# Attention and a convolved feed-forward layer on one core: early steps of three engines put in another order

## The chip, the cores and the metric

The kernel runs on one core of a Trainium2 chip. A core has a matrix engine (TensorE, PE in the profile; its weight loads are shown apart as PEld), three engines for work by element (VectorE = DVE, ScalarE = ACT, GpSimd = POOL) and a sequencer that issues most transfers (SyncE = SP). Each engine takes its instructions in one order and stops at an instruction whose inputs are not there. The metric is the device time of one execution in microseconds (us); the kernel before takes 469.8 us, the median of 469.11, 469.8 and 470.95.

## The reference

Attention in chunks of 64 rows for 8 batches, 8 heads, 576 rows and 64 columns a head, then a feed-forward layer with a convolution of three taps along the sequence and a sigmoid gate:

```python
scores = scale * np.matmul(q_c, k_c.transpose(0, 1, 2, 4, 3))     # chunks of 64 rows
scores = scores - np.max(scores, axis=-1, keepdims=True)
attn = np.exp(scores)
attn = attn / (np.sum(attn, axis=-1, keepdims=True) + 1e-09)
x = np.matmul(attn, v_c)            # heads side by side: 8 x 576 x 512
...
h = np.maximum(x @ w_in, 0.0)       # 512 -> 1024
conv_out[t] = sum of conv_w[k] * h[t - 1 + k] for k in 0, 1, 2
gate = 1.0 / (1.0 + np.exp(-conv_out))
return h * gate @ w_out             # 1024 -> 512
```

The weights come as 64-bit numbers; all results are 32-bit.

## The kernel before

**Attention by tiles.** The 4608 rows are 36 tiles of 128 (t0 to t35). For each of the early ones the loads bring q and k (`load_rows`, L129 and L136) and v (L186). TensorE transposes q and k into PSUM (`t_pe`, L198 and L203, two halves), a copy brings them to SBUF (`t_copy`: L77 on ScalarE, L79 on VectorE), TensorE forms the scores (L250) in a pair of PSUM banks called sx. VectorE takes the maximum and subtracts it (`s_max` L260, `s_sub` L264), ScalarE does the exponential (`s_exp` L269), VectorE the sum (`s_sum` L273), an addition of 1e-9 (`s_eps`, L277 on ScalarE or L279 on VectorE) and the reciprocal (`s_rec` L282); `s_norm` (L322) multiplies, on VectorE or GpSimd. TensorE transposes the result (`p_pe` L329), a copy follows (`p_copy`), and `attn_v` (L342) writes the attention output into the sx pair. It is split into a high and a low part for the next product: `x_hi` (L397, ScalarE) and `x_lo` (L401, VectorE).

**The feed-forward layer by units.** 384 rows make a unit. For each of eight blocks of 128 columns of w_in, `mm1` (L411) makes 12 matmuls (high by high, low by high, high by low) into one of six PSUM banks b0 to b5. `h_relu` (L419) makes the ReLU there, `c_mid` (L449, ScalarE) and `c_left`, `c_right` (L454, VectorE) add the three taps, `c_sig` (L465, ScalarE) is the gate and `c_mul` (L484, VectorE) multiplies; only then is the bank free for another block or a transpose. In the names here c_mul[0,2] is unit 0, block 2. The last product, by w_out, is done with seven products of sums of quarters (`product` L515), whose right sides `f_hi`, `f_lo` (L502) and `f_sum` (L505) prepare.

**The weights.** Six loads for w_in (wi0a to wi3) and four for w_out (wo0 to wo3) go through two slots of SBUF, w0 and w1 (L547). Three steps turn a 64-bit number into a 32-bit one: `w_scale` (L561, ScalarE), `w_shift` (L565, VectorE) and `w_words` (L570, VectorE), and after the last the slot is free for the next load. `w_hi` (L77 or L79) and `w_left` (L574) split the result into its two parts; for w_out there are also `w_diff` (L592 to L594), `w_lo_q` (L587) and, for the sums of quarters, `w_lo_d` (L600).

**What sets the order.** Each of these is a step with an engine, a cost, a list of the steps that it follows, and sometimes other engines that can do it. Two tables of numbers decide. `moved_` (L968) holds 4 x step + n: that step goes to its n-th other engine. `order_` (L997) is a list of all steps; a planner goes through it, gives out the buffers and banks in that order and works out when each step begins on its engine. The steps are then written out in the order of these begins, and each engine's instructions are tied to that order. Where the plan sees TensorE idle before 110 us, it puts filler matmuls on an identity (L1161). A step of GpSimd that uses the SBUF port it shares with VectorE is made to wait for the step of VectorE that `order_` names ahead of it, if the plan has the two at one time.

## Time and profile before

| | before |
|---|---|
| median of 3 runs | 469.8 us |
| profiled execution | 470.28 us, span 468.5 us |
| busy: PE, DVE, ACT, POOL | 456.2, 409.6, 263.7, 283.5 us |
| granted clock of PE | 1.00 in all slices |
| DMA | 64.32 MB, 137 GB/s over the span |

The span is the time from the first to the last instruction that the profiler shows; the profiled execution's own time is 1.8 us longer. In the page, a row of a timeline is a start, a length, an engine and a line, what is written and read, how many instructions; in brackets the idle time of the engine just before, and whose end ended it as far as the profile can tell.

### The profile page before, as it was taken

The page shows a single profiled execution, that of the slowest core. Times are in us where ns is not written, and L with a number is a line of the kernel's source. Part 1 is how long each engine was busy: PE and PEld are TensorE (multiplying, and loading weights), DVE is VectorE, ACT ScalarE, POOL GpSimd, SP SyncE. Part 2 cuts the span into 40 slices and gives each one's busy share as a digit, 9 for nine tenths or more (in the row PEclk, how much of TensorE's full clock was granted, in tenths as well). Part 3 has the DMA queues.
Part 4 walks back from the last instruction along what each step waited for, and adds up shares of the span by engine and source line. Part 5 has one row for each costly group of instructions (what it writes and reads, how often), then busy time and mean ns, then how long its engine had stood idle before and what let it go on. Part 6 is the DMA issues. An engine that isn't in the chain of part 4 may idle for free.

```text
span 468.5 us, 13076 instructions
## 1 busy us (share of the span) xinstructions
PE 456.2 (97%) x5287; PEld 444.3 (95%) x5287; DVE 409.6 (87%) x771; ACT 263.7 (56%) x544; POOL 283.5 (61%) x256
## 2 busy tenths in 40 slices
PE   7899899999999999999999999999999999999996
PEld 7779798999999999999999999999999999999996
DVE  2899999999999899989788889998989987977784
ACT  3589988756646555564444564455556453542641
POOL 0344768847686654979678967755856643448221
PEclk9999999999999999999999999999999999999999
DMA  7999999999896839687987495741215101100012
GB/s 223 248 305 306 246 149 218 158 177 209 147 158 175 191 95 178 126 158 180 181 182 182 109 172 111 169 128 33 58 35 157 25 24 29 40 17 31 22 46 91
DMA packets 184320, 64.32 MB, mean 137 GB/s; under 512 B 155564, under 2 KB 175044, under 8 KB 184260
## 3 DMA queue, kind: packets, MB, share of 16 engines
q1 hardware_dynamic: 184260, 63.48, 62.7%
q8 instruction: 42, 0.69, 0.6%
q14 instruction: 18, 0.15, 0.1%
HBM read 50.88 MB, written 23.59 MB: 159 GB/s over the span
## 4 chain that ended last, share of the span: by engine, by line
PE 80%; DVE 9%; DMA 5%; ACT 2%; issue 1%; SPq 1%; POOL 1%; DVEq 0%; ACTq 0%; POOLq 0%
PE b_ps L411 36%; PE b_ps L515 36%; DVE gt L454 2%; PE sx_ps L250 2%; PE sx_ps L342 2%; PE z_ps L342 2%; DMA v<-in_v 1%; DMA w<-in_moe_w_out 1%; DVE f L502 1%; DMA qk<-in_k 1%; DMA w<-in_moe_conv_w 1%; DVE wt L570 1%; PE z_ps L250 1%; PE b_ps L329 1%; SPq L129 1%
## 5 line engine op out<-in xcount | busy, mean ns | idle before, releaser
L515 PE MATMUL b_ps<-wo_h,f 128*128 128x256 f32 x1008 | 190.9, 282 | 0.4 <-DVE wt L533 0.3
L515 PEld LDWEIGHTS b_ps<-wo_h,f 128*128 128x128 f32 x1008 | 158.8, 188 | 2.0 <-issue 0.5
L515 PE MATMUL b_ps<-wo_l,f 128*128 128x256 f32 x504 | 141.2, 280 | 0.0
L454 DVE SCALAR_TENSOR_TENSOR gt<-b_ps,cw,gt 128x384 f32<-128x384 f32 (+3 forms) x208 | 116.4, 576 | 11.2 <-ACT gt L449 9.1
L502 POOL TENSOR_TENSOR f<-gt,f 128x512 fp32r<-128x512 f32 x67 | 86.4, 1294 | 45.5 <-ACT f L77 16.3
L515 PEld LDWEIGHTS b_ps<-wo_l,f 128*128 128x128 f32 x504 | 94.9, 188 | 0.0
L411 PE MATMUL b_ps<-x_h,wi_h 128*128 128x386 f32 (+2 forms) x384 | 84.6, 342 | 0.0
L411 PE MATMUL b_ps<-x_l,wi_h 128*128 128x386 f32 (+2 forms) x384 | 83.3, 339 | 0.0
L411 PE MATMUL b_ps<-x_h,wi_l 128*128 128x386 f32 (+2 forms) x384 | 83.1, 338 | 0.0
L465 ACT ACTIVATE gt<-gt 128x384 f32<-128x384 f32 (+2 forms) x96 | 49.9, 524 | 54.5 <-DVE gt L454 54.2
L411 PEld LDWEIGHTS b_ps<-x_l,wi_h 128*128 128x128 f32 x384 | 68.8, 188 | 0.0
L411 PEld LDWEIGHTS b_ps<-x_h,wi_l 128*128 128x128 f32 x384 | 68.6, 188 | 0.0
L449 ACT ACTIVATE gt<-b_ps,cw 128x384 f32<-128x384 f32 (+2 forms) x104 | 56.5, 556 | 20.6 <-DVE b_ps L421 18.5
L411 PEld LDWEIGHTS b_ps<-x_h,wi_h 128*128 128x128 f32 x384 | 65.5, 188 | 1.0 <-ACT gt L449 0.2
L505 POOL TENSOR_TENSOR gt<-gt 128x512 f32<-128x512 f32 x41 | 52.8, 1295 | 15.3 <-DVE gb L505 6.0
L484 DVE SCALAR_TENSOR_TENSOR gt<-gt,b_ps 128x192 f32<-128x192 f32 (+2 forms) x120 | 47.2, 410 | 8.8 <-ACT gt L465 8.5
L419 ACT ACTIVATE b_ps<-b_ps 128x386 f32<-128x386 f32 (+2 forms) x79 | 37.6, 479 | 28.2 <-PE b_ps L411 27.0
L79 POOL CAST f<-gt 128x512 fp32r<-128x512 f32 x43 | 26.9, 625 | 21.2 <-PE b_ps L515 18.0
L527 ACT ACTIVATE wt<-b_ps 128x256 f32<-128x256 f32 x54 | 20.6, 381 | 29.8 <-PE b_ps L515 29.7
L77 ACT CAST f<-gt 128x512 fp32r<-128x512 f32 x44 | 26.9, 617 | 14.8 <-PE b_ps L515 8.5
L502 POOL TENSOR_TENSOR f<-gb,f 128x512 fp32r<-128x512 f32 x18 | 23.2, 1294 | 17.9 <-DVE f L502 9.9
L220 DVE STREAM_TRANSPOSE qkT<-qk 128x1024 f32<-128x1024 f32 (+1 forms) x30 | 33.4, 1121 | 0.0
(99 smaller groups left out, 585.6 us busy)
## 6 DMA issues: line engine op xcount, KB each, us to landing
out<-wt SPq DMA_DIRECT2D x36, 256.0 KB, 2.7
qk<-rows SPq DMA_DIRECT2D x24, 320.0 KB, 5.8
rows<-in_q SPq DMA_DIRECT2D x12, 576.0 KB, 8.1
rows<-in_k SPq DMA_DIRECT2D x12, 576.0 KB, 7.8
qk<-rows SPq DMA_DIRECT2D x24, 256.0 KB, 4.6
v<-in_v SPq DMA_DIRECT2D x21, 256.0 KB, 5.0
w<-in_moe_w_out SPq DMA_DIRECT2D x4, 1024.0 KB, 6.5
wt<-wt SPq DMA_DIRECT2D x48, 64.0 KB, 2.0
```

Of the source, the lines that this page charges most:

```text
L77: nc.scalar.copy(out=out, in_=in_)
L79: ENG[eng].tensor_copy(out=out, in_=in_)
L220: nc.vector.transpose(out=to[:, :, i:i + n], in_=of[:, :, o:o + n])
L411: nc.tensor.matmul(h_ps[:, 0:w], lhsT=wt[:, f // 2, kt, P * (f % 2):P * (f % 2) + P], rhs=xt[:, u % NX, kt, 0:w], start=n == 0, stop=n == ...
L419: nc.scalar.activation(out=h, in_=h, func=AF.Relu)
L449: nc.scalar.mul(out=g, in_=h, mul=cw[:, FT + f:FT + f + 1])
L454: nc.vector.scalar_tensor_tensor(out=g, in0=h, scalar=w, in1=g, op0=ALU.mult, op1=ALU.add)
L465: nc.scalar.activation(out=g, in_=g, func=AF.Tanh, scale=0.5)
L484: nc.vector.scalar_tensor_tensor(out=o, in0=g, scalar=1.0, in1=hv, op0=ALU.add, op1=ALU.mult)
L502: ENG[eng].tensor_tensor(out=part(st, 1), in0=quarter(*src), in1=part(st, 0).bitcast(F32), op=ALU.subtract)
L505: ENG[eng].tensor_tensor(out=quarter(*out_), in0=quarter(*a), in1=quarter(*b), op=op)
L515: nc.tensor.matmul(o, lhsT=part(ft, a)[:, j, :], rhs=w[:, i, j, :], start=first and n == 0, stop=n == 3 * FT // 2 - 1, skip_group_check=True)
```

## The change

Only the two tables change, 18 lines of `moved_` and 43 of `order_`; the diff begins

```diff
     moved_ = [
-        89, 113, 141, 165, 186, 225, 353, 505, 793, 801, 817, 969, 977, 1045, 1121, 1129, 1197, 1205, 1465,
...
+        65, 89, 93, 165, 186, 225, 353, 457, 465, 793, 801, 817, 933, 969, 1009, 1045, 1093, 1121, 1129, 1197,
...
     order_ = [
-        84, 85, 103, 87, 88, 0, 104, 18, 1, 86, 2, 105, 3, 90, 4, 5, 89, 91, 6, 122, 92, 19, 20, 7, 106, 107, 8,
...
+        84, 85, 87, 86, 103, 104, 18, 0, 1, 88, 105, 2, 4, 3, 90, 91, 19, 106, 107, 5, 6, 92, 109, 89, 93, 122,
```

The steps of TensorE and the loads keep their order. Other engines take: on VectorE instead of ScalarE one half of t_copy of t3, t4 and t5, and on ScalarE instead of VectorE one of t2 and s_eps of t1; s_norm of t1 goes from GpSimd to VectorE and that of t3 the other way; the first w_left (wi0b) goes from GpSimd to VectorE and that of wi1b the other way; w_hi of wi0a and wi1a change between ScalarE and GpSimd. Some steps of tiles 9 and 10 and of the groups of f near them (s_eps, s_norm, f_lo, f_hi, p_copy, one h_relu) change engines too. The 30 filler matmuls stay 30: three of them go from in front of attn_v of t2 to an earlier place, and three of 512 columns from in front of unit 1's first mm1 to in front of attn_v of t4. VectorE's two lists have the same work behind them at unit 1's c_mul of block 0, but for one s_sum (t8, now later) and the steps that changed engines; behind it the orders differ in short stretches, the last of them near tile 11. Three places follow.

**ScalarE, tiles 2 and 3.** Before; `qkT_266` is tile 3's q and k, of which the two rows are the two halves of t_copy; L561 on `w1_103` is w_scale of wi0a, on `w0_102` that of the load behind it, wi1a; L269 is s_exp of t0 and t1, and p_all is p_copy of t0:

```order
L269 ACTIVATE wt_202<-wt_202 128x512
L269 ACTIVATE wt_246<-wt_246 128x512
L77 COPY qkT_233<-b4_ps_111 128x2x2x2x64
L561 ACTIVATE wt_284<-w1_103 128x512
L77 COPY qkT_266<-b0_ps_107 128x2x2x2x64
L561 ACTIVATE wt_320<-w0_102 128x512
L77 COPY p_all_95<-b1_ps_108 128x512
L77 COPY qkT_266<-b2_ps_109 128x2x2x2x64
```

and now:

```order
L77 COPY qkT_232<-b4_ps_111 128x2x2x2x64
L77 COPY qkT_232<-b5_ps_112 128x2x2x2x64
L269 ACTIVATE wt_263<-wt_263 128x512
L561 ACTIVATE wt_298<-w1_103 128x512
L277 ACTIVATE z_300<-z_300 128x8
L77 COPY p_all_95<-b1_ps_108 128x512
L77 COPY qkT_266<-b2_ps_109 128x2x2x2x64
L561 ACTIVATE wt_330<-w0_102 128x512
```

Before, the second L561 (wi1a) stood ahead of p_copy of t0 and of the second half of tile 3's t_copy; now it stands behind both. The first half of that t_copy is gone from the list, since VectorE has it, and a second row of t2's t_copy (`b5_ps`) and s_eps of t1 (L277) have come.

**ScalarE, tiles 3 to 6.** Before; `w1_103` is the slot of the load wi2, `p_all<-b4_ps` is p_copy of t3, the two qkT rows are tile 6's t_copy, and L277 is s_eps of t4:

```order
L77 COPY p_all_95<-b5_ps_112 128x512
L77 COPY p_all_95<-b4_ps_111 128x512
L397 CAST x_h_90<-sx_ps_75 128x4x128
L397 CAST x_h_90<-sx_ps_75 128x4x2
L269 ACTIVATE wt_493<-wt_493 128x512
L77 COPY qkT_545<-b0_ps_107 128x2x2x2x64
L77 COPY qkT_545<-b1_ps_108 128x2x2x2x64
L561 ACTIVATE wt_591<-w1_103 128x1024
L277 ACTIVATE z_589<-z_589 128x8
L269 ACTIVATE wt_593<-wt_593 128x512
```

and now, with the first h_relu (L419) as the last row:

```order
L77 COPY p_all_95<-b5_ps_112 128x512
L269 ACTIVATE wt_508<-wt_508 128x512
L397 CAST x_h_90<-sx_ps_75 128x4x128
L397 CAST x_h_90<-sx_ps_75 128x4x2
L561 ACTIVATE wt_588<-w1_103 128x1024
L77 COPY p_all_95<-b4_ps_111 128x512
L77 COPY qkT_546<-b2_ps_109 128x2x2x2x64
L277 ACTIVATE z_586<-z_586 128x8
L77 COPY qkT_546<-b1_ps_108 128x2x2x2x64
L269 ACTIVATE wt_590<-wt_590 128x512
L419 ACTIVATE b3_ps_110<-b3_ps_110 128x384
```

L561, w_scale of wi2, came behind p_copy of t3 and both halves of tile 6's t_copy; it now stands ahead of the three, behind x_hi of t2 (L397).

**VectorE, the last weights.** Before, L600 is w_lo_d of wo0, and `wt_968` is the weight tile of wo1 (L565 w_shift, L570 w_words), with s_max and s_sub of t7 (L260, L264) and a c_mul (L484) between:

```order
L454 SCALAR_TENSOR_TENSOR gt_92<-b2_ps_109,cw_94,gt_92 128x383
L600 TENSOR_TENSOR wo_l_89<-wt_833,wo_h_88 128x4x256
L565 TENSOR_SCALAR wt_968<-wt_968 128x1024
L260 TENSOR_REDUCE m_988<-sx_ps_75 128x2x4
L484 SCALAR_TENSOR_TENSOR gt_92<-gt_92,b3_ps_110 128x256
L484 SCALAR_TENSOR_TENSOR gb_93<-gt_92,b3_ps_110 128x127
L264 TENSOR_TENSOR wt_1006<-sx_ps_75,m_988 128x2x4x64
L570 SCALAR_TENSOR_TENSOR wt_968<-w1_103,wt_968 128x1024
```

and now, first around w_words of wo1 (`wt_896`):

```order
L454 SCALAR_TENSOR_TENSOR gt_92<-b1_ps_108,cw_94,gt_92 128x383
L454 SCALAR_TENSOR_TENSOR gt_92<-b0_ps_107,cw_94,gt_92 128x383
L454 SCALAR_TENSOR_TENSOR gt_92<-b3_ps_110,cw_94,gt_92 128x382
L570 SCALAR_TENSOR_TENSOR wt_896<-w1_103,wt_896 128x1024
L454 SCALAR_TENSOR_TENSOR gt_92<-b3_ps_110,cw_94,gt_92 128x383
L484 SCALAR_TENSOR_TENSOR gt_92<-gt_92,b1_ps_108 128x256
L484 SCALAR_TENSOR_TENSOR gb_93<-gt_92,b1_ps_108 128x127
L260 TENSOR_REDUCE m_994<-sx_ps_75 128x2x4
```

and further on, around w_lo_d of wo0; L273 is s_sum of t7, L260 s_max of t8, L282 s_rec of t7, the L484 rows are c_mul of unit 1's blocks 4 and 2, and L502 is the first f_lo:

```order
L273 TENSOR_REDUCE z_1096<-wt_1059 128x8
L600 TENSOR_TENSOR wo_l_89<-wt_822,wo_h_88 128x4x256
L454 SCALAR_TENSOR_TENSOR gt_92<-b2_ps_109,cw_94,gt_92 128x193
L454 SCALAR_TENSOR_TENSOR gt_92<-b2_ps_109,cw_94,gt_92 128x192
L260 TENSOR_REDUCE m_1136<-sx_ps_75 128x2x4
L282 RECIPROCAL z_1096<-z_1096 128x8
L484 SCALAR_TENSOR_TENSOR gb_93<-gt_92,b2_ps_109 128x1
L484 SCALAR_TENSOR_TENSOR gt_92<-gt_92,b2_ps_109 128x192 x2
L484 SCALAR_TENSOR_TENSOR gb_93<-gt_92,b5_ps_112 128x1
L484 SCALAR_TENSOR_TENSOR gt_92<-gt_92,b5_ps_112 128x192 x2
L502 TENSOR_TENSOR f0_1066<-gt_92,f0_1066 128x512
```

w_words of wo1 has moved ahead of s_max and s_sub of t7, and w_lo_d of wo0 from two rows in front of w_shift of wo1 to behind s_sum of t7. The first f_lo, which stood ahead of c_mul of blocks 4 and 2, now follows them.

## Rows read from the trace of the kernel before

**Rows 1.** Page: busy time by engine; chain that ended last, by engine

```profile
PE 456.2 (97%) x5287; PEld 444.3 (95%) x5287; DVE 409.6 (87%) x771; ACT 263.7 (56%) x544; POOL 283.5 (61%) x256
...
PE 80%; DVE 9%; DMA 5%; ACT 2%; issue 1%; SPq 1%; POOL 1%; DVEq 0%; ACTq 0%; POOLq 0%
```

**Rows 2.** Windows: us, busy time by engine (instructions), granted clock, DMA share, GB/s

```profile
12.00:36.00 24.00, 21.24 (x452) 18.14 (x452) 21.45 (x44) 16.74 (x31) 10.47 (x11) 1.00 0.96 278
36.00:48.00 12.00, 12.00 (x132) 11.62 (x131) 11.73 (x21) 11.23 (x24) 5.72 (x7) 1.00 1.03 307
48.00:60.00 12.00, 10.50 (x176) 9.14 (x175) 12.00 (x24) 11.29 (x25) 7.43 (x7) 1.00 0.98 218
60.00:84.00 24.00, 23.01 (x194) 21.83 (x193) 24.00 (x62) 20.80 (x46) 18.39 (x16) 1.00 1.10 194
84.00:468.00 384.00, 379.79 (x4228) 374.73 (x4226) 337.45 (x618) 198.95 (x416) 240.65 (x211) 1.00 0.56 115
```

**Rows 3.** Timeline of PE, 14 to 35 us: start, length, tile, idle before

```profile
21.32 0.46 PE L250 MATMUL sx_ps<-qkT 64*64 64x64 f32 x16 [1.21 <-ACT qkT L77]
...
26.44 1.13 PE L198 MATMUL b_ps<-ident,qk 128*64 128x128 f32 x16 [0.59 <-DMA qk<-in_k]
...
30.99 0.74 PE L1161 MATMUL b_ps<-ident_r 128*128 128x256 f32 x3
```

**Rows 4.** Timeline of ACT, 14 to 37 us

```profile
19.60 0.67 ACT L561 ACTIVATE wt<-w 128x512 f32<-128x512 f32 x1 [2.33 <-DMA w<-in_moe_w_in]
...
20.64 0.63 ACT L77 COPY qkT<-b_ps 128x512 f32<-128x512 f32 x1
...
32.42 0.66 ACT L397 CAST x_h<-sx_ps 128x512 fp32r<-128x512 f32 x2 [0.42 <-PE sx_ps L342]
...
34.89 1.14 ACT L561 ACTIVATE wt<-w 128x1024 f32<-128x1024 f32 x1
...
36.85 0.47 ACT L419 ACTIVATE b_ps<-b_ps 128x384 f32<-128x384 f32 x1
```

**Rows 5.** DMA issues of wi3 (21.6 us) and wi2 (27.4 us): KB, us to landing

```profile
w<-in_moe_w_in SPq DMA_DIRECT2D x1, 1024.0 KB, 8.0
...
w<-in_moe_w_in SPq DMA_DIRECT2D x1, 1024.0 KB, 6.9
```

**Rows 6.** Timeline of PE, 51 to 62 us

```profile
58.65 0.69 PE L342 MATMUL sx_ps<-p_all,v 64*64 64x64 f32 x32 [1.04 <-ACT gt L465]
...
60.15 0.95 PE L1161 MATMUL b_ps<-ident_r 128*128 128x512 f32 x3
```

**Rows 7.** Timeline of DVE, 44 to 80 us

```profile
48.90 1.23 DVE L570 SCALAR_TENSOR_TENSOR wt<-w,wt 128x1024 uint32<-128x1024 uint32 x1
...
63.23 1.21 DVE L600 TENSOR_TENSOR wo_l<-wt,wo_h 128x1024 fp32r<-128x1024 f32 x1
...
66.69 1.51 DVE L570 SCALAR_TENSOR_TENSOR wt<-w,wt 128x1024 uint32<-128x1024 uint32 x1
...
77.06 0.60 DVE L484 SCALAR_TENSOR_TENSOR gt<-gt,b_ps 128x192 f32<-128x192 f32 x2
```

**Rows 8.** Timeline of POOL, 60 to 92 us

```profile
65.12 2.00 POOL L587 TENSOR_TENSOR wo_l<-wt,wo_h 128x256 fp32r<-128x256 f32 x2 [2.01 <-DVE wt L565]
...
74.33 1.99 POOL L587 TENSOR_TENSOR wo_l<-wt,wo_h 128x256 fp32r<-128x256 f32 x2
76.27 1.05 POOL L322 TENSOR_TENSOR wt<-wt,z 128x512 f32<-128x512 f32 x1
```

**Rows 9.** Timeline of PE, 76 to 95 us

```profile
77.81 0.63 PE L329 MATMUL b_ps<-ident,wt 128*128 128x128 f32 x4 [0.99 <-ACT b_ps L419]
...
84.29 0.69 PE L250 MATMUL sx_ps<-qkT 64*64 64x64 f32 x32
```

**Rows 10.** Timeline of DVE, 80 to 85 us

```profile
81.47 0.60 DVE L484 SCALAR_TENSOR_TENSOR gt<-gt,b_ps 128x192 f32<-128x192 f32 x2
82.00 1.23 DVE L220 STREAM_TRANSPOSE qkT<-qk 128x1024 f32<-128x1024 f32 x1
```

94 rows, old and new, of tables (moved_, order_) are left out of this document.

## The prediction, made before the result was known

> **What bounds the kernel now.** I read the busy shares and the chain first: TensorE is busy 456.2 of 468.5 us and 80% of the chain of waits is its own, so a change that leaves TensorE's work and its order alone can give back at most the time in which TensorE stands still [rows 1]. Then I read the windows to see where that is. From 84 us on it is busy 379.79 of 384.00 us, and what the diff changes there stands beside the FFN's products (part 5); before that it stands still 2.76 us in 12 to 36 us (24.00 less 21.24), 0 in 36 to 48, 1.50 in 48 to 60 and 0.99 in 60 to 84 [rows 2]. The granted clock is 1.00 (2.4 GHz) in all of them.
>
> The two early stretches have different limits. In 12 to 36 us the DMA share is 0.96, and the longest waits of TensorE are 1.21 us on ScalarE's copy of tile 3 and 0.59 us on the load of tile 5 [rows 2, 3]. In 36 to 84 us VectorE is the limit: it is busy 11.73, 12.00 and 24.00 us of 12, 12 and 24, that is 0.27 us idle in 48 [rows 2]. There TensorE waits for VectorE's lists of small steps: a PSUM bank is free only after `c_mul` (L484), and the copy of attention's output is done only after `x_lo` (L401). So what this change is worth is decided by whether VectorE's list gets shorter or better ordered between 36 and 84 us, and not by the waits that stand out at 21 us.
>
> **Part 1, 14 to 27 us: the copy of tile 3.** Before, ScalarE stands 2.33 us in front of `w_scale` of wi1a, which waits for its load, and `t_copy[t3,1]` is behind it: it runs 20.64 to 21.27, and TensorE's scores of tile 3 continue at 21.32 after 1.21 us of waiting [rows 3, 4]. Now that copy stands ahead of `w_scale`, and the other copy of tile 3 is done by VectorE. VectorE takes three such copies from ScalarE and gives one, net 2 x about 0.6 us (a copy is 0.63 us on ScalarE [rows 4]), which lie inside its 24.00 - 21.45 = 2.55 us of idle time in this stretch [rows 2]. So the 1.21 us go. But the next transposes wait for tile 5's load, which ends a wait of 0.59 us at 26.44 [rows 3]; the order of the loads is unchanged and the engines of the DMA are 0.96 busy, so I let this load land when it did. Then all of the 1.21 us becomes a longer wait at 26.44: gain 0 of 1.21. If the loads followed the earlier release of their buffers, it would be up to 1.21; that end stays in the range.
>
> **Part 2, 28 to 44 us.** The three filler matmuls at 30.99 (0.74 us) go to an earlier gap [rows 3]. They filled a gap that has other causes: `s_sub` of tile 4 comes one copy later on VectorE (about 0.6 us), so the 0.74 us turns into waiting; I take 0, with 0.74 less 0.6 as the other end. On ScalarE `w_scale` of wi2, which waits for the load of wi2, now stands ahead of `p_copy[t3]`, both copies of tile 6 and `s_eps[t4]`. That load is issued at 27.4 and takes 6.9 us, so it lands at 34.3 [rows 5]. Before, `w_scale` began at 34.89, late enough to find it there [rows 4]. Now ScalarE stands from about 33.1 (the end of `x_hi[t2]`, begun at 32.42) to 34.3, then works off w_scale (1.04 us to the next start), p_copy and two copies (three at about 0.55) and exp (0.55): 34.3 + 1.04 + 1.65 + 0.1 + 0.55 = 37.6, where `h_relu` of the first FFN block started at 36.85 [rows 4]. That is 0.75 us late for VectorE's first conv step. VectorE has the conversion of wi2 to do there and 0.27 us idle [rows 2]; I let it use that work as cover and charge 0. If the cover is gone, the price is 0.75 less 0.27, some 0.5 us.
>
> **Part 3, 44 to 61 us.** VectorE's list here is the same set of steps, permuted: c_mul[0,2], c_mul[0,5] and w_words come at other places. The three 128x512 fillers (0.95 us at 60.15) move in front of attn_v of tile 4 [rows 6]. Since 60.15 to 60.94 was partly covered by the wait for x_hi of tile 6 and the fillers now make attn_v[t4] later by about the same, I count the pair of moves between +0.5 and -0.5 and take 0. The wait of 1.04 us at 58.65 ends with x_lo of tile 5 on VectorE [rows 6]; in the new list about the same sum of steps precedes it, so it stays. At the end of the stretch TensorE stands where it stood, within half a us.
>
> **Part 4, 61 to 84 us, where the gain is.** `w_words` of wo1 ran 66.69 to 68.20 behind w_lo_d of wo0 (1.21 us at 63.23), `s_max`, `s_sub` and two c_mul [rows 7]. Now w_words stands before those and w_lo_d comes eight us later. GpSimd's list hangs on wo1: w_diff, w_lo_q (74.33, 1.99 us), s_norm of tile 7 (76.27 to 77.32), and TensorE's transpose of that tile starts at 77.81 after 0.99 us [rows 8, 9]. Its other input before was the bank that c_mul[1,2] freed on VectorE at 77.06 + 0.60 = 77.66 [rows 7]. Now the bank comes from c_mul[1,4], which stands in front of c_mul[1,2] and no longer has f_lo, c_left[1,0] and s_sub[t8] ahead of it: three steps of about 0.65 us (the c_mul took 0.60), so it ends near 75.7. So GpSimd decides: w_lo_q must now follow w_lo_d on VectorE. Between the end of w_lo_d and 75.7 stand a c_right pair, an s_max, an s_rec and the c_mul itself, some 1.95 us, which puts it at about 73.75. Then 73.75 + 1.94 (from w_lo_q's start to the next one's) + 1.05 = 76.75 for s_norm, and the transpose starts at about 77.0 where it was 77.81. TensorE is 0.8 us ahead when the FFN block before the first product ends.
>
> The next check takes most of it back. VectorE's two lists have done the same work again at c_mul[1,0], which ended at 82.08, and t_dve of tile 9 follows until 83.23 [rows 10]. Now x_lo of tile 7 stands right behind it (128x512; half of the 1.21 us of the 128x1024 subtraction in [rows 7], and a start, so about 0.68), and it is the last reader of the sx bank that the scores of tile 9 write: 82.00 + 1.23 + 0.68 = 83.91. The scores of tile 9 can start at about 83.95; before they started at 84.29 [rows 9]. So 0.8 shrinks to 0.35 us. Bounds: 0 if VectorE is 0.35 us late by then, and 0.99 if c_mul[1,0] moves with TensorE.
>
> **Part 5, after 84 us.** The rest of the diff (s_norm and s_eps of tiles 9 and 10, f_lo and f_hi of two groups, one h_relu) has other engines swap steps beside products that never wait: 0. What TensorE gains by 84 us it keeps, since it is 98.9% busy from there [rows 2].
>
> **Sum.** 0 + 0 + 0 - 0.35 + 0 = -0.35 us. The profiled execution took 470.28 us (span 468.5 and 1.8 around it), so 469.9 for it; it lies 0.5 above the median of the three runs, 469.8, and against that the forecast is 469.45 us.
>
> **One thing the sum leaves out.** VectorE's w_words took 1.51 us at 66.69, while GpSimd's w_lo_q was still running (65.12 to 67.12), and 1.23 us at 48.90; w_lo_d took 1.21 us at 63.23, in GpSimd's 2.01 us of idle time [rows 7, 8]. The Trainium skill's GPSIMD Engine Reference, section Key points, says that GpSimd shares its SBUF interfaces with VectorE and that they contend when a VectorE instruction has two SBUF inputs. The trace agrees, with 1.51 against 1.23. w_lo_d has two SBUF inputs and moves from an idle stretch of GpSimd into a busy one, so by that rule it would lose 0.28 us and the gain would be 0.07; by the rows at its old place it is 0.35.
>
> **Rivals.**
> - *Everything goes.* The waits of 36 to 84 us (1.50 + 0.99 = 2.49 us [rows 2]) vanish and the result is 469.8 - 2.5 = 467.3. For it: the new lists serve the very steps that TensorE waits for. Against it: VectorE has 0.27 us idle in 48 [rows 2], so it can't finish 2.5 us sooner; order alone can only move waits, unless two or more stretches of 0.28 us by GpSimd [rows 7] go too.
> - *Nothing arrives.* The waits change their names: the 0.8 us of part 4 goes to x_lo[t7] or to c_mul[1,0] altogether. 469.8. For it: the 0.35 us left is the difference of sums over 20 steps.
> - *Slower, through ScalarE.* The mechanism is part 2's w_scale at the head of ScalarE's list. The load of wi3 took 8.0 us where that of wi2 took 6.9 [rows 5]. If wi2 takes 8.0 as well, ScalarE is 1.1 us later still, 0.75 + 1.1 = 1.85 us at h_relu; VectorE's 0.27 us and the slack of about 0.5 us at the first banks cover some 0.8, and the other 1.1 us reach TensorE: 469.8 + 1.1 = 470.9. It decides from a landing at about 34.5 on, and would pass 0.5% with one at 36. Against it: nothing in the loads' order changed.
>
> **How the numbers follow.** Chances: forecast 0.46, nothing 0.25, everything 0.13, slower 0.16. Half a per cent, 2.35 us, is about what a measurement of this kernel can tell from no change; the three runs alone lie 1.84 us apart. "Everything" passes that bound in most of its cases (0.11), and a little of the forecast's upper end with part 1's 1.21 us does too (0.01): faster 0.12. The slower rival passes it only with a landing after 36 us: 0.07. The rest, 0.81, is the same. The likeliest case by itself lies between 468.4 (0.99 and half of part 1) and 470.0; the range goes to 467.2 for the first rival and to 471.3 for the last.
>
> **What would show it.** In the changed trace: the scores of tile 3 without a wait at 20 us, and a longer DMA wait at 26.4 (part 1 is wrong if tile 5's transposes start before 26); ScalarE's wait at w_scale until 34.3 and h_relu near 37.6 (part 2); x_lo of tile 5 still ending a wait near 58.5 (part 3); tile 7's transpose near 77.0, limited by s_norm, and the scores of tile 9 near 83.95 with VectorE as releaser (part 4). A start of those scores before 82.5 or after 85 makes the prediction wrong, whatever the total says.

## The result, and the profile after

The changed kernel takes 473.15 us (median of 5 runs, 472.35 to 474.27), the kernel before 469.80 beside it (469.11 to 470.95). The ratio is 1.0063, interval 1.0040 to 1.0086: slower by about 3 us (3.35 between the medians), where 469.45 was forecast and 471.3 was the upper end of the range. The profiled execution took 473.97 us, with a span of 472.2.

The page of the changed kernel, busy time and the chain of waits by engine:

```profile
PE 456.8 (97%) x5287; PEld 444.2 (94%) x5287; DVE 411.6 (87%) x772; ACT 262.7 (56%) x543; POOL 283.9 (60%) x256
...
PE 69%; DVE 16%; DMA 5%; ACT 4%; issue 3%; SPq 1%; POOL 0%; DVEq 0%; ACTq 0%
```

TensorE's work is the same (456.2 before, [rows 1]); VectorE's share of the chain went from 9 to 16%. The windows:

```profile
12.00:36.00 24.00, 20.18 (x448) 17.26 (x448) 21.59 (x44) 13.92 (x26) 9.60 (x11) 1.00 0.92 265
36.00:48.00 12.00, 12.00 (x132) 11.62 (x131) 10.92 (x18) 11.69 (x23) 4.92 (x5) 1.00 0.99 303
48.00:60.00 12.00, 10.55 (x118) 9.22 (x116) 11.77 (x24) 11.57 (x26) 8.58 (x8) 1.00 1.07 245
60.00:84.00 24.00, 22.41 (x234) 21.04 (x238) 23.68 (x60) 19.82 (x43) 17.14 (x15) 1.00 1.03 181
84.00:468.00 384.00, 381.87 (x4260) 376.47 (x4252) 340.57 (x624) 201.27 (x422) 242.88 (x212) 1.00 0.56 113
```

Against [rows 2] the row to look at is the second: VectorE, which was busy 11.73 us of 12, is now busy 10.92, while TensorE, busy all the time, shows nothing there yet. TensorE's steps on which the prediction spoke (start, length, tile, wait before):

```profile
25.22 1.13 PE L198 MATMUL b_ps<-ident,qk 128*64 128x128 f32 x16 [0.31 <-DMA qk<-in_k]
...
52.43 0.86 PE L1161 MATMUL b_ps<-ident_r 128*128 128x512 f32 x3
53.87 0.69 PE L342 MATMUL sx_ps<-p_all,v 64*64 64x64 f32 x32 [0.58 <-DVE x_l L401]
...
60.27 0.69 PE L342 MATMUL sx_ps<-p_all,v 64*64 64x64 f32 x32 [1.02 <-ACT p_all L77]
...
63.09 0.98 PE L411 MATMUL b_ps<-x_h,wi_h 128*128 128x388 f32 x4 [1.08 <-ACT qkT L77]
...
79.16 0.66 PE L329 MATMUL b_ps<-ident,wt 128*128 128x128 f32 x4
...
84.65 0.40 PE L515 MATMUL b_ps<-wo_h,f 128*128 128x256 f32 x1 [0.31 <-DVE gt L484]
...
86.38 0.69 PE L250 MATMUL sx_ps<-qkT 64*64 64x64 f32 x32
...
114.67 0.66 PE L329 MATMUL b_ps<-ident,wt 128*128 128x128 f32 x4 [0.67 <-DVE gb L484]
```

In order: the transposes of tile 5, the fillers and attn_v[t4], attn_v[t6], the first FFN block of unit 1 (mm1[1,3]), the transpose of tile 7 (p_pe[t7]), product[1], the scores of tile 9, p_pe[t10]. A loss shows best in stretches between the same two steps of TensorE, since all that came before cancels. From the starts in the traces, in us; "wi2" is its landing less the start of mm1[0,0]; "idle" is VectorE's in the first stretch (mm1[0,0] to mm1[1,3], some 35 to 63 us):

| run | wi2 | idle | mm1[0,0] to mm1[1,3] | to p_pe[t7] | to mm1[2,6] | to mm1[2,2] | all four |
|---|---|---|---|---|---|---|---|
| before | 0.06 | 0.27 | 26.68 | 16.86 | 18.48 | 21.19 | 83.22 |
| before_again | 0.15 | 0.00 | 26.36 | 16.88 | 18.45 | 21.19 | 82.88 |
| after | 0.50 | 1.31 | 28.00 | 16.07 | 19.34 | 22.07 | 85.48 |
| after_again | 0.44 | 1.18 | 27.90 | 16.06 | 19.37 | 22.06 | 85.39 |

So of some 3 us, 2.2 to 2.6 lie between mm1[0,0] and mm1[2,2]: +1.2 to 1.6, then -0.8, then +0.9 and +0.9. Outside, the kernels don't differ in a settled way: mm1[0,0] starts at 33.3 to 35.5 us in the seven traces of the kernel before and what was made from it, at 33.7 to 35.6 in eleven of the changed kernel and what was made from that (two more, a_hole and a_full, waited 3.68 and 2.47 us for a load and started at 37.5 and 38.0); and from mm1[2,2] to the end it is 350.7 to 351.6 in the former, 350.5 to 351.6 in the latter. The four traces of the table alone do differ ahead of mm1[0,0], by 0.8 to 1.5 us; whether the change does that is left open.

### The profile page after: what moved, and what is told of

Read it like the earlier page. It is cut to its first block, busy times and chain, and to the rows that moved or that the text cites. A ratio compares the mean times of both kernels' runs of the same rounds, so it can differ in the third digit from the quotient of the medians.

```text
span 472.2 us, 13063 instructions
## 1 busy us (share of the span) xinstructions
PE 456.8 (97%) x5287; PEld 444.2 (94%) x5287; DVE 411.6 (87%) x772; ACT 262.7 (56%) x543; POOL 283.9 (60%) x256
## 4 chain that ended last, share of the span: by engine, by line
PE 69%; DVE 16%; DMA 5%; ACT 4%; issue 3%; SPq 1%; POOL 0%; DVEq 0%; ACTq 0%
PE b_ps L411 33%; PE b_ps L515 30%; DVE gt L454 3%; DVE f L502 2%; PE sx_ps L342 2%; DMA w<-in_moe_w_in 2%; PE z_ps L342 1%; DVE gt L484 1%; DMA v<-in_v 1%; DVE z L273 1%; DMA w<-in_moe_conv_w 1%; DVE wt L570 1%; PE sx_ps L250 1%; DVE m L260 1%; DVE wt L264 1%
## 5 line engine op out<-in xcount | busy, mean ns | idle before, releaser
L454 DVE SCALAR_TENSOR_TENSOR gt<-b_ps,cw,gt 128x384 f32<-128x384 f32 (+3 forms) x208 | 116.9, 578 | 12.2 <-ACT gt L449 10.0
L502 POOL TENSOR_TENSOR f<-gt,f 128x512 fp32r<-128x512 f32 x68 | 87.7, 1296 | 47.4 <-ACT f L77 18.4
L484 DVE SCALAR_TENSOR_TENSOR gt<-gt,b_ps 128x192 f32<-128x192 f32 (+2 forms) x120 | 47.2, 411 | 8.8 <-ACT gt L465 8.5
L419 ACT ACTIVATE b_ps<-b_ps 128x386 f32<-128x386 f32 (+2 forms) x80 | 38.2, 480 | 28.6 <-PE b_ps L411 27.4
L502 POOL TENSOR_TENSOR f<-gb,f 128x512 fp32r<-128x512 f32 x17 | 22.0, 1295 | 15.6 <-DVE f L502 7.6
```

The source lines that it names most:

```text
L419: nc.scalar.activation(out=h, in_=h, func=AF.Relu)
L454: nc.vector.scalar_tensor_tensor(out=g, in0=h, scalar=w, in1=g, op0=ALU.mult, op1=ALU.add)
L484: nc.vector.scalar_tensor_tensor(out=o, in0=g, scalar=1.0, in1=hv, op0=ALU.add, op1=ALU.mult)
L502: ENG[eng].tensor_tensor(out=part(st, 1), in0=quarter(*src), in1=part(st, 0).bitcast(F32), op=ALU.subtract)
```

## The experiments

Each kernel has one line more, ahead of `early_banks`, which puts step i right behind step j in the order of issue (on engine e, where one is given); the numbers are those of the planner:

```diff
+    for i, j, e in ((249, 51, None), ): begin[i], end[i], steps[i]['eng'], steps[i]['port'] = begin[j] + 1e-4, begin[j] + 1e-4 + end[i] - begin[i], e or steps[i]['eng'], steps[i]['port'] if not e else e != 'ACT' and steps[i]['fn'] is not t_copy
```

Below only its list stands. Kernels a_ start from the changed kernel, b_ from the one before.

**before_again, after_again**: either kernel once more, nothing edited.

> The kernel before, unchanged, for how far two traces of one kernel agree. Every theory expects the same places within 0.3 us up to 112 us: the first FFN block at 34.3, attn_v of tile 4 at 51.7, the transpose of tile 7 at 77.8, that of tile 10 at 111.6; a total of 469 to 471 us.

> The changed kernel, unchanged, for how far two traces of it agree. Every theory expects the same places within 0.3 us: first FFN block at 35.1, attn_v of tile 4 at 53.9, transpose of tile 7 at 79.2, of tile 10 at 114.7; a total of 472 to 474 us.

468.93 and 472.91 us. The stretches came again within 0.4 and 0.1 us (table).

**b_early, a_early**: the early copies and s_norm of tile 1. In a_early s_norm[t1] runs ahead of its reciprocal, so tile 1's attention is computed from sums not yet inverted.

```diff
+ b_early: (233, 130, 'DVE'), (115, 233, None), (116, 115, 'DVE')   t_copy[t3,0], s_norm[t1] to VectorE
+ a_early: (233, 114, 'ACT'), (116, 17, 'POOL')   the two back
```

> The kernel before with one piece of the change: one half of tile 3's copy and s_norm of tile 1 go to VectorE and stand in front of w_shift and w_words of wi1a. Theory 1 (the loads hang on VectorE): w_words of wi1a ends 0.9 to 1.2 us later (22.4 for 21.45), the load of wi3 is issued as much later (22.5 for 21.69), w_scale of wi3 with all of ScalarE's list behind it and w_words of wi3 are 0.8 us late, and the first FFN block starts near 35.1; 0.8 to 1.4 us slower in all. Rival (ScalarE's own order, w_scale of wi2 ahead of the copies): this kernel does not have that, so the first FFN block starts at 34.3 and the time is that of the kernel before. The prediction on record also expects no loss here.

> The changed kernel with the half of tile 3's copy back on ScalarE and s_norm of tile 1 back on GpSimd. Theory 1 (the loads hang on VectorE): w_words of wi1a ends near 21.2 for 22.4, the load of wi3 is issued near 21.5 for 22.48 and lands at 29.7 for 30.68, TensorE's first FFN block starts 0.8 us sooner (34.3), VectorE's list is 0.8 to 1.4 us sooner at 54 us, and the total is 0.8 to 1.6 us less. Rival (ScalarE's order; x_lo of tile 3): at most 0.3 us less at 54 us.

b_early 470.06, ratio 0.9999 (0.9982 to 1.0015); a_early 472.51, 1.0052 (1.0032 to 1.0071). The time did not move with the early part, so that theory fell. Its steps did come in b_early (the load of wi3 issued at 22.45 us, mm1[0,0] at 35.20), and the time was still that of the kernel before. a_early shows less, since its load of wi3 was issued at 22.79, no sooner than in the changed kernel (22.48).

**b_scale**: w_scale[wi2] ahead of p_copy[t3] and both t_copy[t6] on ScalarE, as the change has it.

```diff
+ (37, 259, None), (246, 37, None)   w_scale[wi2] behind s_exp[t4], p_copy[t3] behind it
```

> The kernel before with only w_scale of wi2 moved ahead of p_copy of tile 3 and the copies of tile 6 on ScalarE. Theory 1 (the loads hang on VectorE): wi2 lands at 34.3 as before, h_relu of the first block is at most 0.75 us late, and TensorE is within 0.3 us of before at attn_v of tile 4 (51.7). Rival (ScalarE's own order): h_relu at 37.6 for 36.85, VectorE's list 0.75 to 1.4 us late behind it, attn_v of tile 4 0.5 to 1.4 us late.

471.49 us (one run; 469.0 to 471.3 in the 13 runs of the kernel before beside it). ScalarE in b_scale waits for wi2, and p_copy[t3], both t_copy[t6] and s_eps[t4] stand behind it:

```profile
35.68 1.15 ACT L561 ACTIVATE wt<-w 128x1024 f32<-128x1024 f32 x1 [1.38 <-DMA w<-in_moe_w_in]
36.73 0.56 ACT L77 COPY p_all<-b_ps 128x512 f32<-128x512 f32 x1
37.20 1.12 ACT L77 COPY qkT<-b_ps 128x512 f32<-128x512 f32 x2
38.20 0.21 ACT L277 ACTIVATE z<-z 128x8 f32<-128x8 f32 x1
```

The first three could have run while it waited: TensorE had ended the last transposes for them at 35.08. The input of s_eps[t4] came at 36.41, from s_sum. VectorE then waits for s_eps[t4]:

```profile
38.44 0.21 DVE L282 RECIPROCAL z<-z 128x8 f32<-128x8 f32 x1 [0.84 <-ACT z L277]
```

Its idle time in the stretch is 0.87 us, and the stretch 27.27 instead of 26.36 to 26.68.

**b_wo1**: w_lo_d[wo0] behind s_sum[t7], and the first f_lo behind c_mul[1,2].

```diff
+ (56, 439, None), (198, 327, None)
```

> The kernel before with only part 4 of the prediction: w_lo_d of wo0 moved behind s_sum of tile 7 and the first f_lo behind c_mul of unit 1's block 2 on VectorE. If part 4 holds: w_words of wo1 ends at 67.0 for 68.2, s_norm of tile 7 ends near 76.6, its transpose starts at 77.0 for 77.81, and 0.4 to 0.8 us of it are left at 112 us. Rival: the wait only changes its name, the transpose starts within 0.2 us of 77.8, or all is given back by 85 us; total that of before.

475.59 us, 1.0127 (1.0099 to 1.0155): much worse, and no test of part 4 by itself. VectorE waits 0.55 us for w_scale[wo1] and 0.99 for GpSimd, and then w_lo_d runs into a collision:

```profile
69.99 3.08 DVE L600 TENSOR_TENSOR wo_l<-wt,wo_h 128x1024 fp32r<-128x1024 f32 x1
```

and GpSimd's beside it:

```profile
69.62 2.36 POOL L600 TENSOR_TENSOR wo_l<-wt,wo_h 128x1024 fp32r<-128x1024 f32 x1 [2.00 <-DVE wt L570]
```

3.08 us for what took 1.21 alone [rows 7]: it ends 1.09 us after GpSimd's end at 71.98, as if nearly all its work came then. TensorE stood 3.08 us for c_mul behind it, and its clock fell (last section).

**a_xlo, a_xf**: x_lo[t3] behind w_words[wo0]; in a_xf the three fillers ahead of attn_v[t4] are left out too.

```diff
+ (249, 51, None)   both
+            for _ in range(0 if i in (266, ) else int(...   a_xf
```

> The changed kernel with x_lo of tile 3 directly behind w_words of wo0 on VectorE, three steps earlier. Theory (this one step holds attn_v of tile 4): x_lo ends at 52.2 for 53.8, attn_v of tile 4 starts at 53.3 behind the fillers, 0.55 us sooner, and the gain is still there at the transpose of tile 7. Rival (VectorE as a whole is late): the gain at attn_v is gone again by the first block of unit 1 (63.1), since other steps of VectorE move back by 0.6 us.

> The changed kernel with x_lo[t3] behind w_words[wo0] on VectorE and the three filler matmuls ahead of attn_v[t4] left out, looked at by its trace. Theory B (the 1.3 us lost between mm1[0,0] and attn_v[t4] are three fillers of about 0.29 us and the 0.58 us wait for x_lo[t3], the one behind the other): the stretch from mm1[0,0] to attn_v[t4], 18.7 to 18.8 us in the changed kernel, comes to 17.4 to 17.6 us. Rival (TensorE waits there for something else that is late, as the run with x_lo[t3] moved alone left it at 18.75): it stays above 18.3 us and attn_v[t4] waits. What comes behind it could take the gain back by a longer wait at mm1[1,3]; then the stretch from mm1[0,0] to mm1[1,3] stays near 28.0 us.

a_xlo 472.51, a_xf 471.85 us (one run each). In a_xlo nothing is gained: attn_v[t4] starts 18.75 us after mm1[0,0] (18.78 changed). TensorE in a_xf:

```profile
51.86 0.69 PE L342 MATMUL sx_ps<-p_all,v 64*64 64x64 f32 x32
...
55.56 0.66 PE L203 MATMUL b_ps<-ident,qk 128*128 128x128 f32 x4 [0.72 <-DVE gb L484]
...
57.90 0.63 PE L329 MATMUL b_ps<-ident,wt 128*128 128x128 f32 x4 [0.47 <-DVE wt L322]
...
62.18 0.97 PE L411 MATMUL b_ps<-x_h,wi_h 128*128 128x388 f32 x4 [1.18 <-ACT qkT L77]
```

attn_v[t4] starts 17.39 us after mm1[0,0], 1.39 sooner than in the changed kernel, as in the one before (17.40). But VectorE makes TensorE wait 0.72 and 0.47 further on: mm1[1,3] starts at 27.71, so 0.29 is kept of 1.39 (0.19 of 1.29 against after_again). The wait at attn_v[t4] was a sign, not the cause.

**a_tail, a_flopool**: the end of the third block.

```diff
+ a_tail: (514, 605, None), (515, 607, None)   c_sig[2,6], c_mul[2,6] earlier
+ a_flopool: (378, 378, 'POOL')   the f_lo at 109 us back on GpSimd
```

> The changed kernel with c_sig and c_mul of unit 2's block 6 moved up by one step on ScalarE and two on VectorE. Theory: the transpose of tile 10 no longer waits 0.67 us for it and starts at 114.0 for 114.67, and TensorE is 0.7 us sooner from there to the end. Rival: another step (o_copy or x_lo of tile 9, which come later on VectorE now) takes its place within 10 us and the gain is given back.

> The changed kernel with one f_lo of the third block (at 108.9 us, 1.58 us on VectorE) back on GpSimd as it was before the change. Theory C: c_mul[2,6] ends about 1.6 us sooner, the 0.67 us wait of p_pe[t10] goes, and the stretch from mm1[2,6] to p_pe[t10] comes from 16.2 to 15.3 to 15.5 us. Rival (GpSimd is then late with this f_lo and the sum behind it, and VectorE or TensorE waits for it instead): p_pe[t10] or p_pe[t11] waits 0.5 us or more and the stretch from mm1[2,6] to p_pe[t11] stays within 0.3 us of 18.1.

a_tail 471.44 (one run): the last stretch is 21.66 us, 0.41 kept of the 0.73 by which p_pe[t10] comes sooner (15.43 us after mm1[2,6] for 16.16). a_flopool 474.08 (one run): 22.33, no gain; TensorE waits 0.38 for GpSimd and 0.42 at p_pe[t10]. Its early part, which is not edited, is told below.

**a_flo**: the first two f_lo one step later on VectorE.

```diff
+ (198, 310, None), (200, 313, None)
```

> The changed kernel with the first two f_lo of VectorE (78.4 and 82.8 us) each moved one step later on VectorE, so that neither starts while a GpSimd instruction runs. Theory C (a VectorE instruction with two SBUF inputs is held until the GpSimd instruction beside it ends): each f_lo comes down from about 1.25 us to about 0.7, product[1] waits no more for c_mul[1,0], and the stretch from p_pe[t7] to mm1[2,6] comes from 19.3 to 18.4 to 18.8 us. Rival (the two f_lo are long for another reason, or the path there is the order of the steps, not their length): they stay above 1.1 us, or the stretch stays above 19.1 us.

471.88 us (one run). VectorE in a_flo, both f_lo:

```profile
77.91 0.68 DVE L502 TENSOR_TENSOR f<-gt,f 128x512 fp32r<-128x512 f32 x1
...
81.65 1.01 DVE L502 TENSOR_TENSOR f<-gt,f 128x512 fp32r<-128x512 f32 x1
```

and TensorE's next wait:

```profile
87.60 0.50 PE L515 MATMUL b_ps<-wo_h,f 128*128 128x256 f32 x2 [0.62 <-POOL f L502]
```

The scores of tile 9 come 0.78 us sooner (6.44 after p_pe[t7], 7.22 changed, 6.48 before), then GpSimd's sums, fed by the later f_lo, take 0.5 back: the stretch to mm1[2,6] is 19.06. The 0.78 is not the collision's alone, since the second f_lo now also stands behind c_mul[1,0], which had waited for it.

**a_best**: a_xf, a_flo, a_flopool and a_tail in one.

> The changed kernel with all the repairs together: x_lo[t3] later and the three fillers gone, the two f_lo of 78 and 83 us one step later, the f_lo of 109 us back on GpSimd, and c_sig and c_mul[2,6] earlier. If the three losses (1.3 us at 52 to 54 us, 0.9 at 79 to 98, 0.9 at 98 to 117) are the whole slowdown and add up, it takes 2.5 to 3 us off the changed kernel: 469.6 to 470.6 us, at the time of the kernel before (ratio to it 0.998 to 1.002). If part 4's 0.8 us at the transpose of tile 7 then survives, it comes out below before, 469.0 to 469.5. Rival (the early loads and ScalarE's order at 18 to 33 us hold the loss): it stays above 471.5.

473.22 us (470.75 to 476.21), 1.0062 (1.0031 to 1.0093): as slow as the changed kernel, and spread wider. All four stretches sum to 84.76, 0.7 below the changed kernel and 1.5 to 1.9 above the one before. The repairs don't add up to the loss.

**a_wi2, a_hole**: other places for w_scale[wi2] in the changed kernel.

```diff
+ a_wi2: (37, 290, None), (38, 37, None)   behind p_copy[t3], both t_copy[t6], s_eps[t4]
+ a_hole: (37, 292, None), (38, 37, None)   behind p_copy[t3], t_copy[t6,1]
```

> The changed kernel with w_scale[wi2] put behind p_copy[t3], both t_copy[t6] and s_eps[t4] on ScalarE, as they stood before the change; nothing else. Theory D: ScalarE's wait of 1.78 us at 34 to 36 us shrinks below 0.6, h_relu[0] comes 0.8 to 1.2 us sooner after mm1[0,0] (3.68 us in the changed kernel, 2.59 before), VectorE's wait of 0.73 us at c_left[0,0] goes, the stretch from mm1[0,0] to mm1[1,3] falls from 28.0 to 27.0 to 27.5, and the time from 473.1 to 472.0 to 472.6, with less spread between runs. Rival (VectorE's and TensorE's own order between 44 and 63 us holds the loss, and ScalarE only follows): the stretch stays above 27.8 and the time within 0.3 us of the changed kernel's.

> The changed kernel with only p_copy[t3] and t_copy[t6,1] put ahead of w_scale[wi2] on ScalarE, so that they fill its wait of 1.78 us for the load, and w_scale[wi2] still starts when wi2 has landed. Theory E (VectorE is the bound from 35 to 63 us, and the hole of 0.95 us there, which ScalarE's wait makes, is most of the loss): VectorE's waits between w_shift[wi2] and c_left[0,0] sum to less than 0.4 us, mm1[1,3] comes 0.6 to 1.0 us sooner after mm1[0,0] (28.0 us in the changed kernel, 26.7 before), and the time falls from 473.1 to about 472.3. Rival (the stretch is held by the later order of VectorE and ScalarE, whatever hole there is): the hole closes and the stretch still takes over 27.7 us. Second rival (another step then waits in the same place, as w_shift[wi2] did): the sum of VectorE's waits from 36 to 42 us stays above 0.8.

a_wi2 473.01, 1.0072 (1.0049 to 1.0094); a_hole 472.83, 1.0051 (1.0029 to 1.0073): neither differs from the changed kernel. In a_wi2 the stretch is 28.33, as its rival had it, and VectorE's next step waits instead, as w_scale now comes too late for it:

```profile
36.96 0.69 DVE L565 TENSOR_SCALAR wt<-wt 128x1024 uint32<-128x1024 uint32 x1 [1.19 <-ACT wt L561]
```

In a_hole the hole closed (0.17 us left) and the stretch is 27.33. But in the profiled run wi2 landed 1.33 us before mm1[0,0], so the hole would have been small anyway: its trace speaks for VectorE as the bound, not for this order as a remedy.

**a_act, a_full**: t_copy[t8,1] ahead of w_scale[wo1]; a_full adds a_wi2, a_xf, a_flo and a_tail.

```diff
+ (452, 305, None), (58, 452, None)
```

> The changed kernel with t_copy[t8,1] on ScalarE put ahead of w_scale[wo1] and c_sig[0,5], nothing else. Theory D: t_copy[t8,1] ends 0.3 to 0.5 us sooner (it can't start before its transposes, 1.1 us after attn_v[t6]) and mm1[1,3], which waits 1.08 us for it, starts as much sooner: the stretch from attn_v[t6] to mm1[1,3] falls from 2.82 to 2.3 to 2.5 us. Rival (mm1[1,3] waits for x_lo[t6], which ended at the same 63.09 us): it stays at 2.8.

> The changed kernel with w_scale[wi2] behind t_copy[t6], x_lo[t3] behind w_words[wo0], the three fillers ahead of attn_v[t4] left out, t_copy[t8,1] ahead of w_scale[wo1], the first two f_lo one step later, c_sig and c_mul[2,6] earlier. Theory D with the earlier findings: the stretch from mm1[0,0] to mm1[1,3] comes to 26.6 to 27.0 us (28.0 changed, 26.7 before), the whole from mm1[0,0] to mm1[2,2] to 83.3 to 84.0 (85.5 changed, 83.2 before), the time to 470.0 to 471.5. Rival (VectorE, busy 97 to 98% of this stretch in either kernel, sets the time, and the changed order leaves it more holes wherever one is closed): the stretch to mm1[1,3] stays above 27.4 and the time above 471.8.

a_act 476.48 (one run), a_full 473.86, 1.0092 (1.0065 to 1.0118). Both edits have a flaw: w_shift[wo1] stands on VectorE ahead of x_lo[t6] and needs w_scale[wo1]. VectorE in a_act:

```profile
64.34 0.69 DVE L565 TENSOR_SCALAR wt<-wt 128x1024 uint32<-128x1024 uint32 x1 [1.89 <-ACT wt L561]
```

The stretch of a_act still answers its question: mm1[1,3] started 0.41 us sooner after attn_v[t6] (2.42 for 2.83), as forecast, and in either kernel 0.05 behind the end of t_copy[t8,1]. So this copy sets that start, and not x_lo[t6], for which the block then stood 0.86 inside. What the start is worth in time these two kernels don't show.

**b_norm, b_norm2**: tile 7's s_norm sooner on GpSimd. In b_norm it was put ahead of s_eps and s_rec as well, so that it scales by sums not yet inverted, and ScalarE waited 4.46 us for it: 474.96 us, 1.0110 (1.0093 to 1.0127), which says nothing on the question. b_norm2 moves w_lo_q[wo1] behind it instead.

```diff
+ b_norm: (442, 62, None)
+ b_norm2: (63, 442, None)
```

> The kernel before with one step moved: s_norm[t7] on GpSimd ahead of both w_lo_q[wo1], where the changed order has it later in its own way. s_rec[t7], which it needs, ended at 74.56 us and GpSimd was then in the first w_lo_q; s_norm[t7] can end at about 75.7 instead of 77.32, and TensorE's wait of 0.99 us for it at the transpose of tile 7 goes. Theory (part 4's step, a gain of 0.8 to 1.0 that is kept to the end where no new work is put on VectorE): the stretch from mm1[1,3] to p_pe[t7] falls from 16.87 to 15.9 to 16.1 us, the time to 468.9 to 469.3, ratio 0.998. Rival (the later w_lo_q and w_lo_d make GpSimd's f_sum or f_lo late and products or scores[t9] wait): what is gained at p_pe[t7] is lost by mm1[2,6], and the time stays within 0.3 us of before.

> The kernel before with one step moved: w_lo_q[wo1] on GpSimd behind s_norm[t7], so that s_norm[t7] starts as soon as s_rec[t7] has ended (74.6 us instead of 76.27). Theory (part 4: TensorE's wait of 0.99 us at the transpose of tile 7 goes, and what VectorE has to do stays the same): the stretch from mm1[1,3] to p_pe[t7] falls from 16.87 to 15.9 to 16.2 us, that from p_pe[t7] to mm1[2,6] stays within 0.4 us of 18.45, and the time comes to 469.3 to 469.9 beside 470.2, ratio 0.998 to 0.9995. Rival (GpSimd's f_sum and f_lo come later, or VectorE sets when product[1] and scores[t9] start, so that TensorE waits there for what it gained): the stretch from p_pe[t7] to mm1[2,6] grows by 0.7 us or more and the ratio is 1.000 within its interval.

b_norm2 470.24, ratio 1.0000 (0.9986 to 1.0015). GpSimd ends s_norm[t7] at 74.86:

```profile
73.82 1.04 POOL L322 TENSOR_TENSOR wt<-wt,z 128x512 f32<-128x512 f32 x1 [0.32 <-DVE z L282]
```

and TensorE waits as long as before:

```profile
76.92 0.63 PE L329 MATMUL b_ps<-ident,wt 128*128 128x128 f32 x4 [0.99 <-ACT b_ps L419]
```

It starts 0.15 us after the end of c_mul[1,2] on VectorE:

```profile
76.17 0.60 DVE L484 SCALAR_TENSOR_TENSOR gt<-gt,b_ps 128x192 f32<-128x192 f32 x2
```

As in the kernel before (77.66 to 77.81, [rows 7, 9]): the bank set that start, not s_norm, and not the h_relu that the profile names. No version tried beats the kernel before.

## Why the prediction was wrong

**Parts 2 and 3, where it failed: forecast 0, measured +1.2 to +1.6.** The step is "VectorE has the conversion of wi2 to do there ...; I let it use that work as cover and charge 0". ScalarE in the changed kernel:

```profile
33.18 0.66 ACT L397 CAST x_h<-sx_ps 128x512 fp32r<-128x512 f32 x2 [0.28 <-PE sx_ps L342]
35.62 1.14 ACT L561 ACTIVATE wt<-w 128x1024 f32<-128x1024 f32 x1 [1.78 <-DMA w<-in_moe_w_in]
36.67 0.57 ACT L77 COPY p_all<-b_ps 128x512 f32<-128x512 f32 x1
...
38.77 0.52 ACT L419 ACTIVATE b_ps<-b_ps 128x384 f32<-128x384 f32 x1
```

wi2 landed at 35.59, not 34.3; h_relu came 3.68 us after mm1[0,0], where it had been 2.59. VectorE has its cover and still stands, since two of its steps wait for ScalarE's late ones:

```profile
37.90 0.20 DVE L282 RECIPROCAL z<-z 128x8 f32<-128x8 f32 x1 [0.22 <-ACT z L277]
38.02 1.18 DVE L570 SCALAR_TENSOR_TENSOR wt<-w,wt 128x1024 uint32<-128x1024 uint32 x1
39.93 0.62 DVE L454 SCALAR_TENSOR_TENSOR gt<-b_ps,cw,gt 128x382 f32<-128x382 f32 x1 [0.73 <-ACT gt L449]
```

Such a hole is not made good. The window of the stretch, before:

```profile
34.26:60.94 26.68, 25.18 (x321) 23.30 (x320) 26.41 (x50) 25.09 (x50) 15.68 (x14) 1.00 1.01 259
```

after:

```profile
35.09:63.09 28.00, 25.21 (x321) 23.22 (x320) 26.68 (x51) 26.65 (x53) 15.52 (x14) 1.00 1.02 256
```

Busy and idle time of any engine add up to the stretch (VectorE: 26.41 + 0.27 and 26.68 + 1.31, with rounding), so the sum alone shows no bound. What shows it is attn_v[t6]: in all 20 traces it starts 0.10 us behind the end of x_lo[t5] on VectorE. In the kernel before (attn_v[t6] at 58.65, [rows 6]):

```profile
57.80 0.75 DVE L401 TENSOR_TENSOR x_l<-sx_ps,x_h 128x512 fp32r<-128x512 f32 x2
```

and in the changed one (60.27):

```profile
58.67 1.49 DVE L401 TENSOR_TENSOR x_l<-sx_ps,x_h 128x512 fp32r<-128x512 f32 x3 [0.20 <-ACT x_h L397]
```

Up to there the path is VectorE's list, as part 3 had it. The table has all traces; "to attn_v[t6]" and VectorE's idle time are counted from mm1[0,0], and "on" is from attn_v[t6] to mm1[1,3]:

| run | wi2 | idle | to attn_v[t6] | less idle | on |
|---|---|---|---|---|---|
| before's order: before | 0.06 | 0.27 | 24.39 | 24.12 | 2.29 |
| before_again | 0.15 | 0.00 | 24.08 | 24.08 | 2.28 |
| b_early | 0.36 | 0.00 | 24.12 | 24.12 | 2.28 |
| b_norm | 0.66 | 0.00 | 24.12 | 24.12 | 2.28 |
| b_wo1 | 0.75 | 0.00 | 24.16 | 24.16 | 2.29 |
| b_norm2 | 1.09 | 0.73 | 24.50 | 23.77 | 2.28 |
| edited here: b_scale | 0.59 | 0.87 | 24.99 | 24.12 | 2.28 |
| changed order: a_tail | -0.14 | 0.95 | 24.66 | 23.71 | 2.83 |
| a_flo | 0.41 | 1.12 | 25.07 | 23.95 | 2.83 |
| after_again | 0.44 | 1.18 | 25.08 | 23.90 | 2.83 |
| after | 0.50 | 1.31 | 25.17 | 23.86 | 2.83 |
| a_early | 2.02 | 2.70 | 26.61 | 23.91 | 2.83 |
| a_flopool | 2.05 | 2.66 | 26.65 | 24.00 | 2.82 |
| edited here: a_hole | -1.33 | 0.76 | 24.50 | 23.74 | 2.83 |
| a_xf | 0.44 | 1.10 | 24.78 | 23.69 | 2.92 |
| a_best | 0.51 | 1.15 | 24.85 | 23.70 | 2.93 |
| a_xlo | 0.75 | 1.36 | 25.15 | 23.79 | 2.89 |
| a_wi2 | 0.46 | 1.55 | 25.50 | 23.96 | 2.83 |
| a_full | -1.15 | 1.37 | 24.86 | 23.48 | 2.42 |
| a_act | not seen | 2.04 | 25.32 | 23.29 | 2.42 |

The changed kernel loses 0.7 to 1.1 us up to attn_v[t6], and not by more work of VectorE: its idle time grew. Of the 1.31 us of idle time 0.95 are the two waits above, behind the late w_scale; 0.30 are two later waits for ScalarE (at 46.61 and 58.67). In the first order a landing up to 0.75 us after mm1[0,0] costs nothing; in the changed one the stretch grows with each later landing, and 0.95 us are idle even where wi2 lands 0.14 us ahead of mm1[0,0] (a_tail). That is the rival "slower, through ScalarE", with nearly its price (1.1 us at TensorE forecast), and it had 0.16. Its condition came in another way (the load took 7.3 us and not 8.0, but was issued later, and landed at 35.59, past the 34.5 from which the rival was to decide), and a_tail shows that it was hardly needed. What I took for against it, that the loads' order is the same, doesn't matter: the same landing is late now, because it is waited for sooner. b_scale, with that move in the kernel before, shows the cause by itself, in one trace (0.87 of idle time, 24.99 for 24.08 to 24.39). That a_wi2, the move back, didn't help has its reason in its own trace, where w_shift[wi2] needs w_scale sooner; which steps would have to move with it is open.

The other part of the loss is "on": 2.83 us from attn_v[t6] to mm1[1,3] for 2.28. Here VectorE is not the bound. TensorE ran the three fillers at this place before, and then mm1[1,3] without a wait; now it waits 1.08 us there for ScalarE's t_copy[t8,1]:

```profile
62.45 0.59 ACT L77 COPY qkT<-b_ps 128x512 f32<-128x512 f32 x1
```

It ends 0.05 us ahead of mm1[1,3] in all 13 traces of the changed order and its edits, and a_act, which ended it sooner, moved that start with it. The pair of moves with the fillers, "between +0.5 and -0.5" and taken as 0, thus came to +0.55 us at this end. Without the fillers at attn_v[t4], and with x_lo[t3] sooner, 0.2 to 0.3 came back (a_xf).

**Part 4, first half: the number right, in part by luck.** Counted from mm1[1,3], tile 7's transpose is 0.8 us ahead (16.07 for 16.87 us), as forecast, by way of c_mul[1,4]'s bank (free at 77.89) and right behind s_norm (79.10); b_norm2 bears out that the bank was what had to come sooner. But mm1[1,3] itself had started 0.55 late. Counted from attn_v[t6] the gain is 0.27 (18.89 for 19.16), and most of the wait of 0.99 us has only moved, to the front of mm1[1,3]. **Second half: forecast 0.35 kept, measured 0.06 at the scores of tile 9, and -0.06 at mm1[2,6].** They started at 86.38, past the 85 that I had set as a mark of being wrong. x_lo[t7] ended 0.05 us ahead of them, as forecast, but TensorE had only just come there: it had waited 0.31 us for c_mul[1,0] at product[1]. c_mul[1,0] ended 5.44 us after p_pe[t7] (4.27 before), and 24.33 after attn_v[t6] (23.42 before). VectorE there:

```profile
78.40 1.25 DVE L502 TENSOR_TENSOR f<-gt,f 128x512 fp32r<-128x512 f32 x1
...
82.78 1.22 DVE L502 TENSOR_TENSOR f<-gt,f 128x512 fp32r<-128x512 f32 x1
83.93 0.14 DVE L484 SCALAR_TENSOR_TENSOR gb<-gt,b_ps 128x1 f32<-128x1 f32 x1
83.99 0.61 DVE L484 SCALAR_TENSOR_TENSOR gt<-gt,b_ps 128x192 f32<-128x192 f32 x2
```

and GpSimd:

```profile
78.05 1.05 POOL L322 TENSOR_TENSOR wt<-wt,z 128x512 f32<-128x512 f32 x1
...
82.15 1.31 POOL L505 TENSOR_TENSOR gt<-gt 128x512 f32<-128x512 f32 x1
```

Both f_lo begin while a GpSimd instruction runs and take 1.25 and 1.22 us; one that begins alone takes 0.68 (a_flo). In the kernel before the two were shorter:

```profile
70.42 0.88 DVE L502 TENSOR_TENSOR f<-gt,f 128x512 fp32r<-128x512 f32 x1
...
80.73 0.76 DVE L502 TENSOR_TENSOR f<-gt,f 128x512 fp32r<-128x512 f32 x1
```

That is 0.83 us more of VectorE, most of the 0.91 by which c_mul[1,0] is late. I had priced such a collision at 0.28, and at w_lo_d only; w_lo_d itself, in its new place, met nothing (1.22).

**Part 5: forecast 0 ("products that never wait"), measured +0.9.** They wait for no product, but p_pe[t10] stands between them and needs c_mul[2,6]'s bank. VectorE lost time again to a collision with GpSimd's f_lo (108.60 to 109.88):

```profile
108.85 1.58 DVE L502 TENSOR_TENSOR f<-gb,f 128x512 fp32r<-128x512 f32 x1
```

and c_mul[2,6] now stands behind t_dve and an output copy; a_tail, which puts it earlier, got 0.41 back. Over the four stretches collisions of this kind, each step counted against the same step alone, cost VectorE some 1.3 us in the kernel before and 3.1 in the changed one.

**Part 1: no gain, as forecast, but for another reason.** Of the 1.21 us in front of the scores of tile 3, 0.41 stayed (a wait for VectorE's copy). Tile 5's transposes start at 25.22, before the 26 that I had set as the mark against it: its load did follow. The time goes at wi3 instead: in 17 of the 19 traces that show its landing mm1[0,0] starts 4.3 to 5.1 us after wi3 lands (30.68 and 35.09 here), and this landing varies from 28.2 to 31.3 us whichever order stands ahead of it.

Sum: 1.2 to 1.6 - 0.8 + 0.9 + 0.9 = 2.2 to 2.6 of about 3 us. The rest, some 0.5, is within what the early loads vary, and not settled.
